# Agent attention and a top-1 mixture of experts in one kernel: the first expert layer issued chunk by chunk, left tiles prepared in sets of two, some VectorE work given to GpSimd, and fewer filler matmuls before the first tile

## The chip, the cores and the metric

The kernel runs on one core of one Trainium2 chip. The metric is device microseconds of one execution; lower is better. Its engines are TensorE (PE, with its weight loads shown as PEld), VectorE (DVE), ScalarE (ACT), GpSimd (POOL) and SyncE (SP, which here issues nearly all DMAs). The program gives each engine its own order of instructions, and they wait on semaphores for one another.

## The reference

The sizes are B = 4 batches, N = 11456 tokens, C = D = 128, 49 agents, E = 8 experts, F = 1024 hidden. Everything is float32.

```python
def sm(a, b):
    s = scale * (a @ b.transpose(0, 2, 1))
    s = s - s.max(-1, keepdims=True)
    e = np.exp(s)
    return e / (e.sum(-1, keepdims=True) + 1e-09)
agent_v = sm(agents, k) @ v            # 49 x 128 for each batch
x = (sm(q, agents) @ agent_v).reshape(B * N, C)
logits = x @ w_gate
e_idx = np.argmax(logits, axis=1)      # one expert for each token
gate_w = softmax(logits)[token, e_idx]
eom = sigmoid(x @ w_output_gate)
for e in range(E):
    mask = e_idx == e
    h = np.maximum(x[mask] @ w1[e], 0.0)
    out[mask] = gate_w[mask, None] * eom[mask, e, None] * (h @ w2[e])
```

## The kernel before

**The work.** A batch is cut into 12 units of 8 columns of 128 tokens (the last has 2 columns of 96), and each unit into one or two *tiles* of 512 tokens: 92 tiles in all. For each batch the kernel first runs over the units of k (scores against the agents, `ks`, and their running maximum), then over those of v (exp of the scores, `ev`; its sum, `sm`; and the product `av`), which gives the 49 averages. `fold` turns them into the weights of the one expert that the batch as a whole prefers, the dominant one: the averages times w1 (`aw`) are split into two float16 parts, `own` and `rest` (tiles `w`), and w2 into `vv`. Then every q unit is scored (`qs`), exponentiated (`ef`), turned by a transposing DMA into `x_ld`, and routed: 8 logits for a token (`lg`), its expert, its gate weight and its output gate (`q_rest`). Every token is sent through the dominant expert, tile by tile. Tokens of another expert are marked on the way (`oht<-oh,ndom`), and worked on again after a phase's batches as *left tiles* of 128 tokens, whose rows replace the first ones: found by counting (`left_table`, `left_index`), gathered from DRAM by indirect DMA, pushed through their own expert in float32 (`let`, `lx`, `lh`, `ly`) and scattered over the output. With these inputs there are 8, 5, 0 and 1 left tiles in the four batches.

**One tile.** Its first layer (`mm1`) makes 8 chunks `h` of 128 hidden values by 512 tokens, in two groups of four. A group takes PSUM banks 0 to 3: four matmuls with `own` (128 rows deep), then four with `rest` (19 rows deep, in four row groups of the array). `relu` follows for each chunk: ACT writes `hh` (float16) and DVE writes what is lost by that, `hl`, and with `hl` the bank is free. The second layer (`mm2`) takes `hh` and `hl` as weights: 8 chunks by 4 columns, each a matmul of 256 columns and one of 128, into banks 4 to 7 (`y`). ACT and DVE add the halves (`ys`, `os`), GpSimd scales (`os<-os,smt`), SP stores.

**What sets the order.** The program is written by a scheduler that runs while the kernel is built. `Clock` holds a model of the time of each engine and of when each buffer is ready; generators (`streams`) each offer their next instruction, and `tick` lets those through that could start by the model's clock, by priority. `main_stream` is the spine: at each step it issues a piece of `mm2`, a whole group of `mm1` if banks 0 to 3 are all free by the model, or, if neither can go, calls `idle`, which lets others through and before the first tile adds a filler matmul (`warm<-idle_x`) if the array has been little used in the last 3413 ns. So what the chip executes is a fixed order for each engine, and where the model was wrong an engine waits, with everything queued behind.

**Before the first tile.** `small_products` goes through `ITEMS`: 12 k units of batch 0, 2 q units, 12 v units, then the q units of batch 0 mixed with k and v of batch 1. `loads` fetches them, 512 KB each, into 8 large places; a place is free once its unit is scored. After each small matmul of these stages `beside` puts a filler of 112 columns into the same PSUM bank (`ks<-idle_x`, `av<-idle_x`, `qs<-idle_x`) until the first tile has started (`clk.started`):

```python
    def beside(t, own):
        if not clk.started:
            PE.matmul(t[:, 512 - SIDE:512], idle_w, idle_x[:, 0:SIDE], start=own, stop=own)
```

**Left tiles.** `PHASES` lists phases as (first batch, batches, left tiles worked on in the main program, table rows). Before, it is batches 0 to 2 with 13 tiles, then batch 3 with 1. `left_prepare` waits until a phase's batches are counted and until the sums of the last batch's v are done, and runs `left_index` twice for the first phase, for 2 tiles and for 11, and once for the second. `left_index` is a chain over SP, DVE and GpSimd: table rows `tbs` and prefix sums into `bigs` by DMA, some twenty small DVE instructions, a gather from `cumd`, more DVE, a gather from `efd`. The order of DVE holds these among the `hl`.

All instructions that go through the recording helpers carry that helper's line, L193 (L203 in the changed kernel), so the profile is read by tile names; buffer and batch numbers are left out of them.

Of the kernel before, what the change touches and what calls it, by code (L numbers as in the profile page):

```python
# [28 lines left out]
PHASES = [(0, 3, 13, 384), (3, 1, 1, 128)]  # L29
NG = B * E  # L30
BIG = 1048576.0
# [17 lines left out]

class Clock:  # L50
# [7 lines left out]
    def __init__(self):  # L58
        self.vt = dict.fromkeys(("PE", "ACT", "DVE", "POOL", "SP", "DMA"), 0.0)
        self.ready, self.read, self.writer, self.before = {}, {}, {}, {}  # L60
        self.slots = [1, 2]
        self.pe = 0.0
        self.psum = set()

        self.apart = {"out"}
        self.recent = []
        self.started = False
# [41 lines left out]
    def issue(self, eng, ins, outs, cost, after):  # L109
        t = max(self.vt[eng], self.at(ins, outs, eng), 0.0 if eng == "PE" else self.now() - 200.0)  # L110
        if eng == "PE":
# [5 lines left out]
            self.pe = 0.0 if wide else cost  # L117
            cost *= slow
# [17 lines left out]
class Engine:  # L136
# [16 lines left out]
    def cost(self, op, ins, outs, k):  # L153
        n = _free(outs[0])
        if self.name == "PE":
# [3 lines left out]
            if not wide and ins[0].shape[0] <= 32:  # L159
                return n / 9.6 + 25.0  # L160
# [82 lines left out]
def agent_attention_top1_moe(ctx, tc, qT, kT, v, aT, wg, wo, w1, w2, cst, out):  # L243
# [51 lines left out]

    def group_free():

        if not all(banks[k][0] for k in range(G4)):
            return None
        return max(when_free(banks[k]) for k in range(G4))  # L300
# [177 lines left out]
    def vacant_turned():  # L478

        return first_place(LARGE, LARGE + SMALL) or first_place(0, LARGE, KEEP)  # L480
# [26 lines left out]
    def loads():  # L507
        for n, item in enumerate(ITEMS):
# [5 lines left out]
            if n == 1:  # L514
                load_constants()

    def beside(t, own):


        if not clk.started:  # L520
            PE.matmul(t[:, 512 - SIDE:512], idle_w, idle_x[:, 0:SIDE], start=own, stop=own)

    def scores(item, name):
# [8 lines left out]
        for t in range(nt):  # L532
            yield from PE.q.matmul(s[0:pp, t * A2:(t + 1) * A2], x[:, t * pp:(t + 1) * pp], at[:, b, :], start=True,
                                   stop=True)
            beside(s, True)
# [8 lines left out]
    def k_unit(b, u):  # L544
        if u == 0:
            K[b] = dict(
                S=wk.tile([P, NCOL, A2], F32, name=f"S{b}", tag="S", bufs=1),
                mx=wk.tile([P, A2], F32, name=f"mx{b}", tag="mx"),
                sm=wk.tile([P, A2], F32, name=f"sm{b}", tag="sme"),
# [5 lines left out]
    def k_rest(b, u, s, mark):  # L555
# [3 lines left out]
        st = sv.rearrange("p (t a) -> p a t", a=A2)  # L559
# [3 lines left out]
        if u == 0:  # L563
            yield from DVE.q.tensor_reduce(mx, st, axis=AX.X, op=ALU.max)
            release(mark)
        else:
            m1 = wk.tile([P, A2], F32, name=f"m1_{b}_{u}", tag="m1")
            yield from DVE.q.tensor_reduce(m1[0:pp], st, axis=AX.X, op=ALU.max)
            release(mark)
            yield from DVE.q.tensor_tensor(mx[0:pp], mx[0:pp], m1[0:pp], op=ALU.max)  # L570
# [4 lines left out]
    def k_max(b):  # L575
        K[b]["M"] = yield from bcast_max(K[b]["mx"], A2, f"km{b}")
# [6 lines left out]
    def v_weights(b, u):  # L583
# [11 lines left out]
        yield from (DVE if b == 0 and u % 3 == 0 else POOL).q.tensor_tensor(e, sv, M[0:pp].unsqueeze(1).broadcast_to([pp, nt, A2]), op=ALU.subtract)  # L595
# [4 lines left out]
    def v_sum(b, u, e):  # L600
        base, pp, nt = UNITS[u]
        sm = K[b]["sm"]
        st = e.rearrange("p t a -> p a t")
        while K[b]["s"] < u:
            yield None
        if u == 0:
            yield from DVE.q.tensor_reduce(sm, st, axis=AX.X, op=ALU.add)
        else:
            m1 = wk.tile([P, A2], F32, name=f"s1_{b}_{u}", tag="m1")
            yield from DVE.q.tensor_reduce(m1[0:pp], st, axis=AX.X, op=ALU.add)  # L610
            yield from DVE.q.tensor_tensor(sm[0:pp], sm[0:pp], m1[0:pp], op=ALU.add)
# [4 lines left out]
    def v_unit(b, u):  # L616
# [12 lines left out]
        for t in range(nt):  # L629
# [3 lines left out]
            if not last_:  # L633
                beside(avp, False)
# [19 lines left out]
    def averages(b):  # L654

        yield from wait_free()
        den = bank(f"den{b}")
        mark = hold()
        yield from PE.q.matmul(den[:, 0:A2], ones, K[b]["sm"], start=True, stop=True)
# [6 lines left out]
    def fold(b):  # L666
# [37 lines left out]
        picking[0] = False  # L704
# [27 lines left out]
        yield from SY.q.dma_start(avnd[b], avn[0:A])  # L732

# [98 lines left out]
    def q_unit(b, u):  # L832
        s, mark = yield from scores(("q", b, u), f"qs{b}_{u}")
        spawn(q_rest(b, u, s, mark))
# [10 lines left out]
    def q_rest(b, u, s, mark):  # L845
# [61 lines left out]
        yield from DVE.q.tensor_tensor(l, L, rr.unsqueeze(2).broadcast_to([pp, nt, 16]), op=ALU.mult)  # L907
# [614 lines left out]
```

## Time and profile before

| | |
|---|---|
| median of 3 runs | 1072.67 us (1071.23 to 1074.8) |
| the profiled execution | 1073.62 us, span of the trace 1071.6 us, mean granted TensorE clock 0.984 |
| busy | PE 1033.2, PEld 840.9, DVE 859.9, ACT 592.6, POOL 275.2 us |
| first `ks` matmul | 7.74 us |
| first `av` matmul, end of the last one | 37.36, 61.2 us |
| first `h` and first `y` matmul | 85.03, 87.7 us |
| last matmul ends | 1060.97 us |
| moved by DMA | 147.13 MB, 137 GB/s in the mean |

Times within the execution count from the trace's first instruction. A row of the timeline gives start, duration, engine, tiles and how many instructions were merged, and in brackets how long the engine was idle before it and who ended that. A row of the windows gives, for a stretch, the busy time and count of each engine, the granted TensorE clock (1 is full, 0.5 half), the busy share of the DMA engines and their GB/s. A float32 matmul shows as two records. Records of matmuls overlap, so how long one takes is the distance from its start to the next start, not its duration.

### The profile page before, as it was taken

The numbers are of one execution on the slowest core, as the hardware profiler recorded it, in microseconds if no ns is written. First come the engines' busy times: TensorE is split into PE (matmuls) and PEld (weight loads), VectorE is DVE, ScalarE is ACT, GpSimd is POOL, SyncE is SP. The second block draws the span as 40 slices with busy tenths as digits, with TensorE's granted clock in tenths as the row PEclk, the third lists the DMA queues.
The fourth block names the chain that finished last, engine by engine and source line by source line (L and its number), as shares of the span: only waits on it lengthen the run. The fifth ranks groups of instructions, "written<-read, shape, count | busy, mean of one in ns | idle before, by whom it ended". The sixth has DMA issues, their size and how long they took to land. (4 is left out here: it accounts for less than half of the span.)

```text
span 1071.6 us, 27654 instructions
## 1 busy us (share of the span) xinstructions
PE 1033.2 (96%) x10671; PEld 840.9 (78%) x10671; DVE 859.9 (80%) x2344; ACT 592.6 (55%) x1396; POOL 275.2 (26%) x440
## 2 busy tenths in 40 slices
PE   9989899999999999999999999999899999999996
PEld 9977777788788877778788788777677676788885
DVE  2738699888988898888988888989989978877551
ACT  2325456565755665556755665556645554655552
POOL 0301123222121232232121232321123263521121
PEclk9999899999999999999999999999999998999998
DMA  8785854444557444453466544446232732644430
GB/s 293 231 213 156 193 117 146 125 122 136 133 141 197 141 134 112 119 147 116 111 185 166 153 125 119 129 123 171 73 75 56 168 92 78 149 136 130 131 124 28
DMA packets 108818, 147.13 MB, mean 137 GB/s; under 512 B 61128, under 2 KB 71548, under 8 KB 108682
## 3 DMA queue, kind: packets, MB, share of 16 engines
q1 hardware_dynamic: 107338, 143.83, 48.4%
q0 software_dynamic: 1344, 1.49, 0.8%
q8 instruction: 85, 1.39, 0.5%
q14 instruction: 51, 0.42, 0.1%
HBM read 91.86 MB, written 35.17 MB: 119 GB/s over the span
## 5 line engine op out<-in xcount | busy, mean ns | idle before, releaser
L193 PE MATMUL y<-vv,hh 128*128 128x256 f16 (+1 forms) x2880 | 593.0, 275 | 4.3 <-DVE w L193 3.1
L193 PE MATMUL y<-vv,hl 128*128 128x128 f16 (+1 forms) x2880 | 532.7, 220 | 3.3 <-DVE hl L193 2.5
L193 DVE SCALAR_TENSOR_TENSOR hl<-h,hh 128x512 f16<-128x512 f32 (+1 forms) x736 | 447.0, 667 | 85.3 <-ACT hh L193 84.2
L193 ACT ACTIVATE hh<-h 128x512 f16<-128x512 f32 (+1 forms) x736 | 372.2, 591 | 231.3 <-PE h L193 231.0
L193 PEld LDWEIGHTS <-hh 128*128 128x128 f16 (+1 forms) x2880 | 284.7, 99 | 67.0 <-issue 37.1
L193 PEld LDWEIGHTS <-hl 128*128 128x128 f16 (+1 forms) x2880 | 320.7, 112 | 10.9 <-DVE hl L193 6.2
L193 PE MATMUL h<-x_ld,w 128*128 128x512 f16 (+1 forms) x1472 | 289.4, 379 | 12.1 <-DVE hl L193 11.5
L193 PEld LDWEIGHTS <-w 128*128 128x128 f16 x1472 | 98.3, 103 | 105.0 <-issue 84.7
L193 POOL TENSOR_TENSOR os<-os,smt 128x512 f32<-128x512 f32 (+1 forms) x92 | 94.3, 1025 | 234.8 <-issue 168.9
L193 ACT COPY ys<-y 128x256 f32<-128x256 f32 x180 | 67.4, 374 | 99.6 <-PE y L193 97.4
L193 PEld LDWEIGHTS qs<-at,q_ld 128*128 128x128 f32 x720 | 112.0, 190 | 7.0 <-DVE km_m L193 0.3
L193 PE MATMUL qs<-at,q_ld 128*128 128x50 f32 x720 | 114.0, 245 | 0.0
L193 PE MATMUL ks<-at,k_ld 128*128 128x50 f32 x720 | 111.4, 257 | 2.2 <-DMA k_ld<-kT 2.2
L193 PEld LDWEIGHTS ks<-at,k_ld 128*128 128x128 f32 x720 | 109.2, 195 | 5.5 <-DMA k_ld<-kT 3.1
L193 PE MATMUL av<-ev,v_ld 128*128 128x50 f32 x720 | 110.7, 251 | 0.0
L193 PEld LDWEIGHTS av<-ev,v_ld 128*128 128x128 f32 x720 | 107.6, 191 | 1.8 <-ACT ev L193 0.2
L193 DVE TENSOR_TENSOR os<-y,ys 128x256 f32<-128x256 f32 x180 | 75.0, 417 | 30.3 <-ACT ys L193 22.4
L193 POOL TENSOR_TENSOR e<-ef,e 128x392 f16<-128x392 f32 (+1 forms) x48 | 41.8, 870 | 151.9 <-ACT e L193 93.4
L193 POOL TENSOR_TENSOR ev<-S,km_o 128x400 f32<-128x400 f32 (+1 forms) x44 | 41.1, 935 | 150.7 <-PE av L193 108.6
L193 POOL TENSOR_SCALAR smt<-lT,i 128x8 f32<-128x8 f32 (+1 forms) x48 | 14.8, 309 | 130.6 <-DVE lT L193 109.9
L193 PEld LDWEIGHTS <-idle_x 128*128 128x128 f16 x305 | 45.9, 158 | 2.7 <-DVE idle_x L193 1.1
L193 PE MATMUL lh<-lxs,lw 128*128 128x128 f32 x224 | 42.9, 276 | 0.0
(200 smaller groups left out, 1041.3 us busy)
## 6 DMA issues: line engine op xcount, KB each, us to landing
q_ld<-qT SPq DMA_DIRECT2D x44, 512.0 KB
v_ld<-v SPq DMA_DIRECT2D x44, 512.0 KB
out<-os SPq DMA_DIRECT2D x88, 256.0 KB
k_ld<-kT SPq DMA_DIRECT2D x43, 512.0 KB
lw<-w SPq DMA_DIRECT2D x28, 512.0 KB
efd<-ef SPq DMA_DIRECT2D x44, 200.0 KB
x_ld<-x_ld SPq DMA_DIRECT2D x176, 38.0 KB
w1t<-w SPq DMA_DIRECT2D x8, 256.0 KB
```

The source lines that it names most:

```text
L193: return getattr(self.eng, op)(*a, **k)
```

## The change

**Fillers and first loads.** `beside` is gone. `filler` puts one matmul of 256 columns into an idle bank after every fourth small matmul until the first tile starts. Loads may run ahead of the first expert choice to item 2 NU + 8 (was + 4), but then stop until the model says that batch 0's w2 has landed (`unpick`). Batch 0's `second`, which squares w2 on ACT, waits until both halves of `w` are written.

**First layer.** `mm1` issues one `own` chunk per call if that one bank is free; the fourth call also issues the four `rest` matmuls. The lead of the first layer over the second, `OFF`, is 10 chunks (was 8).

**DVE and GpSimd.** The maximum of k and the sum of `ev` are kept as 8 x 50 running elementwise maxima and sums and reduced once per batch (`m1`, `s1`); the sums of batches 1 to 3 run on GpSimd, those of batch 0 on DVE. Three of the routing instructions (`ll`, `ld`, `og`) move from DVE to GpSimd. Of batch 0's `ev` subtractions DVE takes every fourth (was third).

**Left tiles.** The phases are now batches 0 and 1 with 13 tiles, and batches 2 and 3 with 1. Indices are made in sets of two tiles, at most two sets alive, in a buffer of their own, and a phase starts as soon as its batches are counted.

**The model.** An instruction of PE, GpSimd or SP that reads what SP loaded is held back another 2000 ns once the first tile has started (`LANDS`); the first `rest` matmul of a group costs 121 ns instead of 25; the last batch's q units may run 8 units ahead (`LAST`, was 5), and q units above 2 of a later batch wait for that batch's `w`.

```diff
-PHASES = [(0, 3, 13, 384), (3, 1, 1, 128)]
+PHASES = [(0, 2, 13, 256), (2, 2, 1, 256)]
+SET = 2
+LANDS = 2000.0
...
-                t = max(t, self.ready.get(x.name, 0.0) + (0.0 if self.writer.get(x.name) in (eng, "PE") else late))
+                w = self.writer.get(x.name)
+                t = max(t, self.ready.get(x.name, 0.0) + (0.0 if w in (eng, "PE") else late + LANDS if late and w == "SP" else late))
...
+    def filler():
+        few[0] += 1
+        if not clk.started and few[0] % 4 == 0:
+            k = idle_bank()
+            if k is not None:
+                PE.matmul(bank("warm", k=k)[:, 0:2 * P], idle_w, idle_x, start=True, stop=True)
...
-        yield from ACT.q.copy(S[0:pp, 8 * u:8 * u + nt, :].rearrange("p t a -> p (t a)"), sv)
-            yield from DVE.q.tensor_reduce(m1[0:pp], st, axis=AX.X, op=ALU.max)
-            yield from DVE.q.tensor_tensor(mx[0:pp], mx[0:pp], m1[0:pp], op=ALU.max)
+        yield from ACT.q.copy(Su.rearrange("p t a -> p (t a)"), sv)
+        if u > 0:
+            yield from DVE.q.tensor_tensor(mx[0:pp, 0:nt], sv.rearrange("p (t a) -> p t a", a=A2),
+                                           S[0:pp, 0:nt, :] if u == 1 else mx[0:pp, 0:nt], op=ALU.max)
...
-            yield from DVE.q.tensor_reduce(m1[0:pp], st, axis=AX.X, op=ALU.add)
-            yield from DVE.q.tensor_tensor(sm[0:pp], sm[0:pp], m1[0:pp], op=ALU.add)
+            yield from (DVE if b == 0 else POOL).q.tensor_tensor(sm[0:pp, 0:nt], sm[0:pp, 0:nt], e, op=ALU.add)
...
+    def unpick(w2t):
+        yield from pause(clk.ready[w2t.name] - clk.now())
+        picking[0] = False
...
+        while b == 0 and len(state[b]["w"]) < 2:
+            yield None
...
-        yield from DVE.q.tensor_tensor(l, L, rr.unsqueeze(2).broadcast_to([pp, nt, 16]), op=ALU.mult)
+        yield from POOL.q.tensor_tensor(l, L, rr.unsqueeze(2).broadcast_to([pp, nt, 16]), op=ALU.mult)
...
-        p = []
-        for g in range(G4):
-            p.append((bank(f"h{i}_{hf}_{g}", k=g), hold()))
-            PE.matmul(p[g][0][:, 0:w], own_[:, g * P:(g + 1) * P], x1, start=True, stop=False)
-            if g < G4 - 1:
-                tick()
+        g = len(group)
+        group.append((bank(f"h{i}_{hf}_{g}", k=g), hold()))
+        PE.matmul(group[g][0][:, 0:w], own_[:, g * P:(g + 1) * P], x1, start=True, stop=False)
+        if g < G4 - 1:
+            tick()
+            return
...
-            if can2 and (G4 * m1 > NB * i + (NB * k + f) / (tiles[i][4] // 2) + OFF or not can1):
+            if can2 and (m1 > NB * i + (NB * k + f) / (tiles[i][4] // 2) + OFF or not can1):
...
-            for i, n in [(0, 2), (2, nst - 2)] if nst > 2 else [(0, nst)]:
+        for i in range(0, nst, SET):
+            n = min(SET, nst - i)
+            sets.append(n)
+            while len(sets) > 2 and sets[-3] > 0:
                 yield None
```

Three places of the built order follow, as they stand in the two programs.

On PE, in the k stage of batch 0, with `ks` the scores and `idle_x` the filler's operand, before:

```order
L193 MATMUL ks_9_458<-at,k_9_ld 128x50
L193 LDWEIGHTS idle_x
L193 MATMUL ks_9_458<-idle_x 128x112
L193 MATMUL ks_9_458<-at,k_9_ld 128x50
L193 LDWEIGHTS idle_x
L193 MATMUL ks_9_458<-idle_x 128x112
```

and now:

```order
L203 MATMUL ks_2_290<-at,k_2_ld 128x50 x4
L203 LDWEIGHTS idle_x
L203 MATMUL warm<-idle_x 128x256
L203 MATMUL ks_2_290<-at,k_2_ld 128x50 x4
L203 LDWEIGHTS idle_x
L203 MATMUL warm<-idle_x 128x256
```

A filler stood beside every small matmul; now one or two stand behind every four. Up to the first `h`, 217 fillers of 112 columns are gone, and fillers of 256 columns go from 52 to 118: the 20 ahead of the first k unit stay, 37 stand in the k stage, 7 among the two q units, 35 in the v stage and 19 behind it. The k, q and v matmuls ahead of the first `h` number 229 before and 228 now.

On ACT, where batch 0's first weights are made (`wsq` squares w1, `vv` with `sq` squares w2, `whi` is the high part of a quarter of the first layer's weights), before:

```order
L193 ACTIVATE wsq_1_1059,sq_945<-w1t_938 128x512
L193 ACTIVATE vv_0_1085,sq_1084<-w2t_941 128x4x128
L193 COPY avn_sb_1082<-avn_1080 49x128
L193 ACTIVATE whi_0_1092<-aw_0_955,s_s 128x512
L193 ACTIVATE vv_1_1087,sq_1084<-w2t_941 128x4x128
L193 ACTIVATE whi_1_1107<-aw_1_1057,s1d_1083 128x512
```

and now:

```order
L203 COPY avn_sb_992<-avn_990 49x128
L203 ACTIVATE whi_0_997<-aw_0_882,s_s 128x512
L203 ACTIVATE whi_1_1011<-aw_1_948,s1d_993 128x512
L203 ACTIVATE whi_2_1017<-aw_2_957,s_s 128x512
L203 COPY S_854<-ks_2_1002 128x400
L203 ACTIVATE whi_3_1031<-aw_3_961,s1d_993 128x512
L203 ACTIVATE vv_0_1049,sq_994<-w2t_872 128x4x128
```

The two squares of w2 stood ahead of and between the `whi`; now they stand behind all four.

On PE in the middle of batch 1, a group of the first layer before (`w_3` is `own`, `w_2` the first `rest`):

```order
L193 MATMUL y_1_8621<-vv_0_4860,hl_1_8368 128x128
L193 LDWEIGHTS w_3_5004
L193 MATMUL h_1_0_8636<-x_7_ld,w_3_5004 128x512
L193 LDWEIGHTS w_3_5004
L193 MATMUL h_1_1_8638<-x_7_ld,w_3_5004 128x512
L193 LDWEIGHTS w_3_5004
L193 MATMUL h_1_2_8642<-x_7_ld,w_3_5004 128x512
L193 LDWEIGHTS w_3_5004
L193 MATMUL h_1_3_8645<-x_7_ld,w_3_5004 128x512
L193 LDWEIGHTS w_2_4979
```

and now, from the second chunk of a group to the third:

```order
L203 MATMUL h_0_1_8696<-x_8_ld,w_1_4786 128x512
L203 LDWEIGHTS hh_7_8445
L203 MATMUL y_1_8628<-vv_1_4557,hh_7_8445 128x256
L203 LDWEIGHTS hl_7_8446
L203 MATMUL y_1_8628<-vv_1_4557,hl_7_8446 128x128
L203 LDWEIGHTS hh_7_8445
L203 MATMUL y_1_8628<-vv_1_4557,hh_7_8445 128x256
L203 LDWEIGHTS hl_7_8446
L203 MATMUL y_1_8628<-vv_1_4557,hl_7_8446 128x128
L203 LDWEIGHTS w_1_4786
L203 MATMUL h_0_2_8704<-x_8_ld,w_1_4786 128x512
```

The four `own` matmuls of a group stood together; now pieces of the second layer stand between them. In the same order the left tiles of the first phase stand between tiles 50 and 79 (of 92), where before they stood from tile 74 to the end; one left tile remains near tile 88.

More of the change, by code (lines that the diff above doesn't have):

```diff
@@ L62, in __init__ @@
         self.pe = 0.0
+        self.rows = False
         self.psum = set()
@@ L515, in loads @@
                 load_constants()
-    def beside(t, own):
-        if not clk.started:
-            PE.matmul(t[:, 512 - SIDE:512], idle_w, idle_x[:, 0:SIDE], start=own, stop=own)
+        loaded.append(True)
+    loaded = []
+    def filler():
[4 more added lines that the diff above has]
+                PE.matmul(bank("warm", k=k)[:, 0:2 * P], idle_w, idle_x, start=True, stop=True)
+    few = [0]
     def scores(item, name):
```

128 lines of the change are left out of this document (64 added, 64 removed).

## The prediction

> **What bounds the kernel now.** I read the page first, then windows over the stages, then the waits of PE, then the timeline wherever one of them pointed. The page's first part names PE:
>
> ```profile
> PE 1033.2 (96%) x10671; PEld 840.9 (78%) x10671; DVE 859.9 (80%) x2344; ACT 592.6 (55%) x1396; POOL 275.2 (26%) x440
> ```
>
> A busy PE is not yet a useful one. Until the first `h` at 85.03 us it computes small matmuls and fillers. The windows of that part, cut at the first `ks` matmul, the first `qs`, the first and last `av`, and the weights (columns: stretch, its length, busy us and count of PE, PEld, DVE, ACT, POOL, granted clock, DMA share, GB/s):
>
> ```profile
> 7.74:31.60 23.86, 23.86 (x272) 23.86 (x271) 7.65 (x19) 5.31 (x13) 1.57 (x4) 1.00 0.90 310
> 31.60:37.36 5.76, 5.59 (x60) 5.15 (x59) 4.37 (x11) 1.61 (x5) 2.01 (x2) 1.00 0.89 310
> 37.36:61.20 23.84, 23.84 (x263) 23.84 (x261) 17.08 (x42) 6.67 (x14) 8.06 (x11) 1.00 0.84 170
> 61.20:69.20 8.00, 7.40 (x90) 6.79 (x89) 4.12 (x23) 1.52 (x6) 0.24 (x1) 1.00 0.30 94
> 69.20:73.30 4.10, 4.09 (x12) 1.82 (x12) 0.96 (x7) 1.19 (x4) 0.00 (x0) 1.00 0.93 314
> 73.30:75.50 2.20, 0.00 (x0) 0.00 (x0) 0.00 (x0) 0.72 (x2) 0.00 (x0) 1.00 1.03 382
> 75.50:85.03 9.53, 9.50 (x68) 8.95 (x69) 7.13 (x19) 5.85 (x12) 1.01 (x2) 0.64 0.91 346
> ```
>
> In the k stage (first row) and the v stage (third row) PE is busy without a gap, so it sets the pace there, with its fillers. After 61.2 the path leaves PE: a chain over DVE, SP's loads of w1, ACT and DVE makes the first weights, and PE idles or runs at a clock of 0.64. From the first `y` at 87.7 to 1060.97 PE is the bound; what can be won there are its waits:
>
> ```profile
> PE h L193 <- DVE hl L193: 11.5, 33, 3.6
> PE lg L193 <- DMA x_ld<-e: 3.7, 1, 3.7
> PE y L193 <- DVE w L193: 3.1, 1, 3.1
> PE ks L193 <- DMA k_ld<-kT: 2.2, 1, 2.2
> ```
>
> **The k and v stages.** The timeline shows what a filler costs there, and a row from mid-run what a small matmul costs alone:
>
> ```profile
> 8.21 0.38 PE L193 MATMUL ks<-at,k_ld 128*128 128x50 f32 x2
> 8.43 0.21 PE L193 MATMUL ks<-idle_x 128*128 128x112 f16 x1
> 8.48 0.38 PE L193 MATMUL ks<-at,k_ld 128*128 128x50 f32 x2
> ...
> 443.70 0.27 PE L193 MATMUL y<-vv,hh 128*128 128x256 f16 x1
> 443.81 0.22 PE L193 MATMUL y<-vv,hl 128*128 128x128 f16 x1
> ...
> 388.55 0.32 PE L193 MATMUL qs<-at,q_ld 128*128 128x50 f32 x2
> 388.70 0.38 PE L193 MATMUL h<-x_ld,w 128*128 128x512 f16 x1
> ```
>
> From 8.21 to 8.48 a small matmul with its filler takes 0.27 us; alone (388.55 to 388.70) it takes 0.15 to 0.16; a matmul of 256 columns takes 0.11 (443.70 to 443.81). Each stage has 90 small matmuls: 90 x 0.27 = 24.3, about the 23.86 and 23.84 of the rows. After, the k stage is 90 x 0.16 + 37 x 0.11 = 18.5 and the v stage 90 x 0.16 + 35 x 0.11 = 18.3, so 5.4 and 5.5 us less. What could be late next is the loads. The DMA engines at their fullest moved this much:
>
> ```profile
> 10.00:15.00 5.00, 5.00 (x58) 5.00 (x58) 1.54 (x4) 1.68 (x5) 0.00 (x0) 1.00 1.03 410
> ```
>
> 512 KB at 410 GB/s is 1.3 us, and a unit of eight matmuls with its three fillers will take 1.6, so PE still sets the pace, narrowly; if the loads got only the 310 GB/s of the k stage's row, a unit would take 1.7 and the two stages would give back some 2 us. The making of `ev` hides too: its subtraction takes 0.99 us on GpSimd, in a row below, which is less than 1.6.
>
> Between the stages lies the chain maximum, transpose, `km_o`, `ev`: the 5.76 us of the second row. The q units' matmuls that cover it shrink, so the chain itself now decides. It gains one reduce per batch:
>
> ```profile
> L193 DVE TENSOR_REDUCE s<-ev 128x50 f32<-128x400 f32 x40 | 33.7, 843 | 2.1 <-ACT ev L193 2.0
> L193 DVE TENSOR_REDUCE m<-ks 128x50 f32<-128x400 f32 x40 | 22.8, 570 | 15.2 <-ACT S L193 15.1
> L193 POOL TENSOR_TENSOR ev<-S,km_o 128x400 f32<-128x400 f32 x40 | 39.6, 991 | 143.8 <-PE av L193 101.7 <-DVE km_o L193 38.7 <-DVE sm L193 2.9
> L193 POOL TENSOR_TENSOR oht<-oh,ndom 128x64 f32<-128x64 f32 x44 | 14.3, 324 | 0.0
> ```
>
> A reduce of 400 elements from SBUF takes 0.84, and about 0.25 is saved on the last unit's own reduce: +0.6. Together the v stage ends 10.3 us earlier, at 50.9.
>
> **From the last av to the first y.** The 8.0 us up to the loaded w1 are a chain and stay; with fewer fillers PE idles in it. Then ACT:
>
> ```profile
> 74.23 0.63 ACT L193 ACTIVATE vv<-w2t 128x512 f16<-128x512 f32 x1 [3.84 <-DMA w2t<-w]
> 76.31 0.68 ACT L193 ACTIVATE whi<-aw,s_s 128x512 f16<-128x512 f32 x1
> ...
> 72.99 0.16 DVE L193 TENSOR_TENSOR s1d<-s_s,kc 128x1 f32<-128x1 f32 x1
> 77.03 0.75 DVE L193 SCALAR_TENSOR_TENSOR w<-aw,s_s,whi 128x512 f16<-128x512 f32 x1 [3.88 <-ACT whi L193]
> ```
>
> The scale was there at about 73.1, and `whi` waited until 76.31 behind a square of w2 that waited for its load. With the squares moved behind, `whi` can start at 73.1; two `whi` (0.68 each, overlapping with DVE) and two `w` (0.75 each) later, at about 75.3, the first group has its weights, against 85.03 before. I put `h` at 75.7 on this old scale, since PE has some 2 us of k matmuls and fillers ahead of it: 9.3 us less. Of that 2.2 come back: `vv` is now late, since its squares, total, scale, ACT and DVE parts (0.63 + 0.63 + 0.7 + 0.4 + 0.65 + 0.75, with hops between) follow the last `whi`, so the first `y` comes 4.9 us behind the first `h`, not 2.67. PE uses 1.3 of these for 8 q matmuls that it owed anyway. Net: 8.4.
>
> The clock takes a part back. After the 2.2 us in which PE had nothing to do (sixth row above), the seventh shows a clock of 0.64, and the idle time ahead of w1 will be as long: about 8.0 minus 5 us of work left there. I charge 2.5 us, half of a 5 us stretch at half clock. The Trainium skill says in "TensorE: Matmul & The Clock Gate", Part 1, that the clock falls only after an idle window of some 3.4 us, and advises against idle gaps over about 3 us; by that the charge would be nothing and the start another 2.5 us shorter. This trace disagrees with it: 2.2 us were enough.
>
> The start, then: 10.3 + 8.4 - 2.5 = **16 us less**, between 8 (PE idle more, loads at 310 GB/s) and 20.
>
> **Waits of the main part.** The 33 waits of `h` for `hl` look like this:
>
> ```profile
> 388.11 0.59 PE L193 MATMUL h<-x_ld,w 128*128 128x512 f16 x2
> ...
> 444.15 0.38 PE L193 MATMUL h<-x_ld,w 128*128 128x512 f16 x1
> 444.75 0.38 PE L193 MATMUL h<-x_ld,w 128*128 128x512 f16 x1 [0.22 <-DVE hl L193]
> ```
>
> Two chunks back to back take 0.59, so 0.21 apart; in a group that was begun before DVE had freed its banks they are 0.60 apart, which loses 0.39 though only 0.22 shows as idle. About 29 of the 33 are of this kind: 11 us. Issued one by one, with second-layer matmuls between, most chunks find their bank free; I keep three quarters, **8 us**, between 2 and 11.
>
> The wait of `lg` for a turned tile (3.7 us, at 123.8) and the half clock behind it fall if the extra 2 us that the model now allows a load are honoured:
>
> ```profile
> 125.00:130.00 5.00, 2.57 (x24) 2.51 (x25) 0.62 (x4) 0.66 (x2) 0.00 (x0) 0.57 0.72 248
> 130.00:135.00 5.00, 5.00 (x41) 3.15 (x40) 3.77 (x14) 2.92 (x8) 0.00 (x0) 0.75 0.70 226
> ```
>
> The clock lost 5 x 0.43 + 5 x 0.25 = 3.4 us, so the place cost 7.1; I take **4** of it, between 0 and 7. For the wait of `y` for `w` (3.1, at the start of batch 3) I find no edit that must remove it: 0.
>
> **Left tiles.** Their index chain puts DVE instructions that wait for a DMA among the `hl`, and PE starves behind them:
>
> ```profile
> 798.02 0.43 DVE L193 TENSOR_TENSOR bigs<-bigs,lrs 128x256 f32<-128x256 f32 x1 [3.41 <-DMA out<-os]
> ...
> 884.61 1.19 DVE L193 TENSOR_TENSOR bigs<-bigs,lppxs 128x990 f32<-128x990 f32 x1 [6.16 <-DMA bigs<-cumd,lrus]
> ...
> 780.00:800.00 20.00, 18.67 (x207) 15.26 (x206) 15.88 (x54) 10.03 (x28) 4.00 (x7) 1.00 0.36 91
> 800.00:820.00 20.00, 17.76 (x163) 12.48 (x163) 17.95 (x57) 10.17 (x24) 6.18 (x10) 0.91 0.25 59
> 880.00:900.00 20.00, 16.13 (x137) 10.79 (x134) 13.40 (x33) 6.75 (x15) 2.54 (x3) 0.83 0.16 45
> 1000.00:1020.00 20.00, 20.00 (x195) 16.65 (x194) 12.40 (x37) 10.62 (x25) 4.00 (x4) 1.00 0.40 131
> ```
>
> The first set (2 tiles) cost 1.33 + 2.24 of idle PE and 0.09 x 20 of clock, 5.4; the set of 11 cost 3.9 + 3.4 = 7.3; the last, of one tile, nothing: 12.7 in all. Now there are eight sets of at most two, each between 0 and 5.4, so 0 to 43. The long wait belonged to eleven gathers in a row, which are gone, and DVE has more room: the 48 units lose a reduce of 0.57 for a maximum of about the same length without the small one behind it, 33 sums of 0.84 and three routing instructions each leave it. I take 1.2 a set, nearer to the set that cost nothing, 10 in all: **3 us less**, between -12.7 and +30.
>
> **GpSimd and the end.** GpSimd gets 33 additions of 0.99 and 144 routing instructions between the 0.32 of `oht` and 0.99, the nearest rows; at 0.4 that is 33 + 58 = 91 us, on top of 275 of 1071. It stays idle two thirds of the time and PE reads nothing of it soon: 0, with the rival below. At the end the last `y` lose the float32 matmuls of left tiles that filled their gaps: +1.5, between 0 and 3.
>
> **Sum.** -16 - 8 - 4 - 3 + 1.5 = -29.5. The page's own execution took 1073.62 us, 0.95 above the median, so 1044.1 there and about **1043 us** as a median. About 0.3% is what a measurement of this kernel can tell from no change.
>
> **Rivals.**
>
> *The start gains little* (15%). The path before the first tile moves from PE to the chains and loads, and the clock halves in the longer gaps. For it: PE is the only thing removed, and the DMA share was 0.84 to 0.90 already. Against it: 410 GB/s were reached. The start gives 8 and the rest 13.5: 1051.
>
> *The stalls go altogether* (15%). Chunk by chunk all 11 us go, the 7.1 of `lg` too, and sets of two cost nothing as the last set of one did (-12.7), with 16 from the start: 16 + 11 + 7 + 12.7 - 1.5 = 45, so 1028.
>
> *DVE waits for others more often* (12%, two thirds of it slower than before). Two edits put waits into DVE's fixed order with `hl` behind them: the eight sets, and routing, where `lm`, `lr` and `ogs` on DVE now read what GpSimd has just written, 144 times. If each set cost the 5.4 of the dearest small one, 43 - 10 = +33; if in addition one hop in twelve starved PE for the 1.33 us of the row at 780, 12 x 1.33 = +16. Then 1043 + 49 = 1092; it turns the sign from +29.5 on. Against it: sets without cost exist, and DVE sheds some 90 us of its 860.
>
> *The chunks do not do what they say* (8%). PE meets the same unfinished `hl` one by one instead of in a group: the 8 us stay, 1051.
>
> The forecast has 50%. Its own range is 1031 to 1057; the stalls' case pulls the lower end down and the DVE case the upper one up, so I give 1022 to 1064. Faster by over 0.3%: all cases but two thirds of the DVE one and a little of the tails, 0.90; within 0.3%: 0.03; slower: 0.07.
>
> **What would show it.** First `h` near 67 and first `y` near 71 to 73 us instead of 85.03 and 87.7; k and v stages of 18 to 19 us with PE busy throughout, or PE waiting for `k_ld` and `v_ld` (then the loads were the bound). `whi` directly behind the scale on ACT. Waits of `h` for `hl` well under 11.5 us. Rows `bigs` on DVE with waits for DMA, and the PE windows around them, tell what the sets cost; waits of DVE for GpSimd's `ll`, `ld`, `og` tell the third rival. I would be wrong if the first `y` came after 80 us, or if the windows between 540 and 800 us showed PE idle by more than a microsecond in twenty.

## The result and the profile after

| | before | after |
|---|---|---|
| median | 1072.33 us (4 runs, 1071.23 to 1074.8) | 1149.15 us (4 runs, 1135.67 to 1151.59) |
| ratio | | 1.069, 95% interval 1.060 to 1.077 |
| profiled execution, clock | 1073.62 us, 0.984 | 1151.59 us, 0.947 |
| first `av`, first `aw` | 37.36, 69.17 us | 37.89, 93.19 us |
| first `h`, first `y` | 85.03, 87.7 us | 101.48, 108.7 us |

The kernel is 77 us slower where 29 faster was forecast. The windows of the start, cut at the same events as before (first `ks`, first `qs`, first `av`):

```profile
7.90:30.40 22.50, 22.50 (x220) 22.34 (x218) 5.17 (x9) 5.55 (x13) 1.57 (x4) 1.00 0.94 338
30.40:37.90 7.50, 6.87 (x47) 6.56 (x47) 5.05 (x11) 2.32 (x6) 3.52 (x4) 0.73 0.69 240
37.90:61.00 23.10, 23.10 (x119) 22.91 (x119) 8.63 (x19) 4.49 (x9) 6.59 (x9) 0.50 0.45 130
61.00:80.00 19.00, 19.00 (x99) 18.82 (x98) 3.82 (x11) 1.36 (x3) 1.76 (x3) 0.50 0.84 164
80.00:93.20 13.20, 13.20 (x81) 13.08 (x81) 3.51 (x20) 1.84 (x7) 0.25 (x1) 0.50 0.48 156
```

The k stage got only 1.4 us shorter, and from the chain behind it the clock stands at one half, with PE busy all the time: the v stage (first to last `av`) takes 42.2 us instead of 23.7. Behind the first `y` the trace runs level with that of before up to 550 us; then come windows like these:

```profile
580.00:600.00 20.00, 13.80 (x153) 12.64 (x153) 8.33 (x29) 6.35 (x18) 3.40 (x6) 0.84 0.58 158
600.00:620.00 20.00, 18.82 (x180) 15.16 (x179) 16.73 (x54) 9.46 (x22) 5.88 (x12) 0.90 0.41 108
620.00:640.00 20.00, 15.02 (x140) 11.34 (x137) 10.56 (x29) 8.61 (x20) 6.77 (x11) 0.83 0.53 175
```

The waits of PE and of DVE name the place, and DVE's timeline shows it. Loads of a left set (`tbs` its table rows, `bigs<-ppid` its prefix sums) hold DVE, with `hl` behind them; GpSimd's routing (`ogs`) holds it for less:

```profile
PE h L203 <- DVE hl L203: 25.6, 25, 4.6
```

```profile
DVE bigs L203 <- DMA bigs<-ppid: 21.8, 8, 4.7
DVE lrs L203 <- DMA tbs<-ttd: 15.8, 4, 5.6
...
DVE ogs L203 <- POOL og L203: 7.5, 8, 2.2
```

```profile
590.84 0.23 DVE L203 TENSOR_SCALAR lrs<-tbs,kc 128x2 f32<-128x2 f32 x1 [4.58 <-DMA tbs<-ttd]
...
596.66 0.42 DVE L203 TENSOR_TENSOR bigs<-bigs,lrs 128x256 f32<-128x256 f32 x1 [3.88 <-DMA bigs<-ppid]
...
599.52 2.47 DVE L203 SCALAR_TENSOR_TENSOR hl<-h,hh 128x512 f16<-128x512 f32 x4
```

To compare kernels I split the stretch from the first `y` to the last: time in which no matmul record runs (idle), half of the busy time inside stretches at half clock, and what is left, the work. The fourth column is the time lost ahead of `own` matmuls of `h`: each one's distance from the matmul ahead of it, less what is usual (the median) for that pair of kinds; it is good to some 3 us.

```
                               length   idle  half clock   work   lost ahead of own h
before                          971.4   23.7      9.3     938.4      19.7
after                          1028.6   53.5     19.7     955.4      57.8
before + chunks                 995.2   39.4     11.7     944.1      54.9
before + eight sets            1006.5   44.0     20.2     942.3      16.8
before + LAST = 8              1007.7   46.6     16.8     944.2      25.8
the best version (below)        959.3   17.6      3.2     938.5       9.0
```

Of the profiled execution's 78 us, 21 lie ahead of the first `y`, and 57 behind it: 30 idle, 10 clock, 17 in the work. What makes up the 17 is open; it may be small waits inside the records. Executions of one program can lie 15 to 24 us apart, by whether the clock halves in the v stage as here (three of these four, by their mean clock); the ratios of single parts below are of executions where it doesn't.

### The profile page after: what moved, and what is told of

It reads as the page before. It is cut to its first block, busy times and chain, and to the rows that moved or that the text cites. A ratio compares the mean times of both kernels' runs of the same rounds, so it can differ in the third digit from the quotient of the medians.

```text
span 1149.8 us, 27405 instructions
## 1 busy us (share of the span) xinstructions
PE 1081.5 (94%) x10520; PEld 876.5 (76%) x10520; DVE 810.0 (70%) x2193; ACT 594.9 (52%) x1396; POOL 353.1 (31%) x627
## 5 line engine op out<-in xcount | busy, mean ns | idle before, releaser
L203 PE MATMUL y<-vv,hh 128*128 128x256 f16 (+1 forms) x2880 | 643.3, 276 | 15.6 <-DVE avs L203 3.8
L203 PE MATMUL y<-vv,hl 128*128 128x128 f16 (+1 forms) x2880 | 560.4, 221 | 0.0
L203 PEld LDWEIGHTS <-hh 128*128 128x128 f16 (+1 forms) x2880 | 294.2, 102 | 107.3 <-issue 70.8
L203 PE MATMUL h<-x_ld,w 128*128 128x512 f16 (+1 forms) x1472 | 338.5, 382 | 30.9 <-DVE hl L203 25.6
L203 PEld LDWEIGHTS <-hl 128*128 128x128 f16 (+1 forms) x2880 | 332.0, 115 | 40.6 <-issue 7.2
L203 PEld LDWEIGHTS <-w 128*128 128x128 f16 x1472 | 92.1, 95 | 57.4 <-issue 50.0
L203 PEld LDWEIGHTS av<-ev,v_ld 128*128 128x128 f32 x720 | 127.6, 230 | 9.6 <-issue 7.3
L203 PE MATMUL av<-ev,v_ld 128*128 128x50 f32 x720 | 127.5, 284 | 0.0
L203 ACT ACTIVATE ev<-ev 128x400 f32<-128x400 f32 (+1 forms) x48 | 25.1, 523 | 37.4 <-POOL ev L203 31.0
L203 PE MATMUL ly<-lw,lh 128*128 128x128 f32 x224 | 42.8, 276 | 0.5 <-DVE os L203 0.5
```

Of the source, the lines that this page charges most:

```text
L203: return getattr(self.eng, op)(*a, **k)
```

## The experiments

Theories: **A**, thin fillers let the clock fall and stay at half; **B**, the sets' loads hold DVE and starve PE; **C**, DVE waits for GpSimd's routing; **D**, chunks hold the banks longer. Three more came later, on the edits of order: **E**, the loads of w1 set when the first weights are made; **F**, the 2 us more for a load (`LANDS`) move instructions into worse places; **G**, the new gates of the q units do it.

**Undoing parts in the changed kernel.** The old fillers again (each small matmul with `beside`, as in the listing of before):

```diff
-            filler()
+            beside(s, True)
```

> The changed kernel with the fillers of before: 112 columns beside every small matmul instead of 256 columns at every fourth. Theory A (thin fillers let the clock fall at 33.9 us and keep it at half up to 95.3): the clock stays at 1.00 through the v stage, the first h comes at 74 to 80 us instead of 101.5, and the time falls by 20 to 27 from 1149 to about 1125, with the stalls from 570 to 900 us left as they are. Rival (the clock falls because of the 0.6 us pause between the stages, whatever fills the rest): the first h stays later than 95 and the time within 5 us of the changed kernel.

Measured: 1136.08 us (1.060, 1.057 to 1.062). In its profile the clock held through the v stage and the first `h` came at 86.3 us (not at 74 to 80, since `aw` waited 6.4 us for its load of w1), but one of its four executions took 1159.83 us, at a mean clock of 0.948 against 0.971 to 0.977. So A is half right: the fillers do not decide it alone. Routing back to DVE:

```diff
-        yield from POOL.q.tensor_tensor(l, L, rr.unsqueeze(2).broadcast_to([pp, nt, 16]), op=ALU.mult)
+        yield from DVE.q.tensor_tensor(l, L, rr.unsqueeze(2).broadcast_to([pp, nt, 16]), op=ALU.mult)
```

(and `ld`, `og` likewise.)

> The changed kernel with the three routing instructions (ll, ld, og) back on DVE. Theory C (DVE waits for GpSimd's routing with hl behind it): the time falls by 15 or more, and the idle time of PE between 570 and 900 us shrinks by a third or more. Theory B (the sets): within 8 us of the changed kernel, the waits for tbs and bigs<-ppid the same in size.

Measured: 1167.13 us (1.083, 1.074 to 1.092), 18 slower than the changed kernel; C fell. Waits of `h` for `hl` grew from 25.6 to 46.6 us. The sets' DVE instructions later, with the thin fillers left in, was to test B alone; its order of instructions ended in a deadlock, so there is no time for it. With the old fillers, the sets' DVE instructions later (by 5 us of the schedule's time) and the sets one after the other:

```diff
+        if nm[0] != "d":
+            yield from pause(5000.0)
         big = wk.tile([P, SET * (2 * P + 12)], F32, name=f"big{nm}", tag="big")
...
+        if nm[0] != "d":
+            yield from pause(5000.0)
         r = col("r")
```

> The changed kernel with the fillers of before and with the later DVE instructions of the sets, both edits at once. Theories A and B together: the gains add, 50 to 70 us, to 1080 to 1100. If the two are one cause (PE's clock, which once low makes every wait longer), less than the sum of the two runs alone by 10 or more.

Measured: 1143.73 us (1.069, 1.064 to 1.073). Up to 570 us each engine's order is that of the run with the old fillers alone, and yet its profile has the clock at half from 35.8 us for 64.9. Between 570 and 960 us DVE's waits for `bigs<-ppid` fell from 17.6 us in that run to 5.7, those for `tbs` from 16.3 to nothing that is listed, and those for `bigs<-cumd` rose from 4.6 to 11.0: part of the wait moves on. From the first to the last `y` it took 1018.1 us instead of 1029.5, so the spreading gained 11 us there, and the clock of the start took them back. Groups of four again, the sets new:

```diff
-    OFF = 10
+    OFF = 8
...
-        group.append((bank(f"h{i}_{hf}_{g}", k=g), hold()))
+            p.append((bank(f"h{i}_{hf}_{g}", k=g), hold()))
```

> The changed kernel with the first layer begun in groups of four again, lead 8, as before. Theory D (chunk by chunk a group of four is spread over 3.4 us instead of 1.3, so 1.8 us instead of 3.6 are left to ACT and DVE to empty its first bank, and every delay of DVE reaches PE): the time lost ahead of own-row h matmuls falls from 58 us to 35 or less, the last rest-row h to the next group's first own-row h grows back to about 3.6 us, and the time falls by 20 or more, to 1130 or less. Theory B alone (the sets' waits are long enough to starve PE either way): the time falls by less than 8.

Measured: 1143.11 us (1.060, 1.054 to 1.066). The time lost ahead of own `h` fell to 9.1 us as D says, the total by only 6. What took its place is not shown: the profiled execution took 1162.46 us, 19 above the median, and has 61.5 us idle in all and 37 lost to half clock.

> The changed kernel with the left tiles as before: phases of three batches and one, sets of 2, 11 and 1 after the last batch's sums. Theory B: the stalls between 570 and 900 us go and those of before (12.7 us) come back, 30 to 45 us less, 1105 to 1120. Theory D: the steady waits of own-row h (14 us in the first 1300 y against 9 before) stay, and the sets' long waits cost more than in the kernel before; the time falls by 15 to 30.

Measured: 1107.62 us, an indication only, since it computes part of the output wrongly. Up to 550 us PE's order is that of the changed kernel, chunks and q edits are in it, and only the left tiles differ; yet the stretch from first to last `y` was 969.8 us, as long as before (971.4), against 1028.6 in the changed kernel. So, as far as this run may be trusted, the sets carry the whole loss behind the first `y` there, and what another part costs depends on the order that it stands in.

> Both: groups of four and the left tiles as before; the start, the fillers, the sums and the routing on GpSimd stay changed. If B and D are the whole cause behind the first y, the time is the kernel before plus what the start costs (15 where the clock stays at half through the v stage, about 0 where not) less what the sums and the routing give: 1065 to 1090. If something else costs there, over 1095.

Measured: 1124.72 us (1.041, 1.033 to 1.049). Over 1095: something else costs. In its profile (1135.17 us, the longest of its four executions) it lay between 740 and 1010 us, far from the start's edits.

**Single parts on the kernel before.** Undoing one of several causes leaves the others to fill its place, so the parts were added singly. Each price below holds for the order of the kernel before.

> The kernel before with one edit, the first layer chunk by chunk with a lead of 10. Theory D: the group's spread grows from 1.3 to about 3.4 us, the time lost ahead of own-row h grows from 20 us to 35 or more, and the kernel is slower by 12 to 30. The forecast on record: 8 us faster (2 to 11).

Measured: 1100.49 us (1.022, 1.017 to 1.027): **24 slower**, D holds. A group of the first layer in this run, and the start of the next:

```profile
441.08 0.38 PE L193 MATMUL h<-x_ld,w 128*128 128x512 f16 x1
...
441.67 0.38 PE L193 MATMUL h<-x_ld,w 128*128 128x512 f16 x1
...
442.27 0.38 PE L193 MATMUL h<-x_ld,w 128*128 128x512 f16 x1
...
443.15 0.71 PE L193 MATMUL h<-x_ld,w 128*128 128x512 f16 x5
...
445.25 0.38 PE L193 MATMUL h<-x_ld,w 128*128 128x512 f16 x1
```

The fourth chunk and its four `rest` matmuls come 2 us behind the first, and only then may ACT and DVE start on the first bank. Over the 184 groups the median from a group's first `own` to its last `rest` grew from 1.28 to 3.06 us, and from there to the next group's first `own` it shrank from 3.63 to 1.82 us, while four `hl` take 2.48. DVE had slack of a microsecond; now its delays reach PE more often (43 waits, 26.1 us, where the kernel before has 33 and 11.5):

```profile
PE h L193 <- DVE hl L193: 26.1, 43, 3.5
```

This run was 15 us behind the kernel before at 477 us. The changed kernel, which has the chunks too but less work on DVE, was level there, and 6 us behind the best version below, so chunks seem to cost less where DVE has room.

The thin fillers alone:

> The kernel before with one edit, the thin fillers (256 columns at every fourth small matmul instead of 112 at each). Theory A: in most executions the clock falls between the k and the v stage and stays at half up to the weights: first h later than 95 us instead of 85.0, the time 8 to 20 above the kernel before; an execution whose clock does not fall there lies within 5 of it. The forecast on record: 10.9 us faster.

Measured: 1075.85 us (1.001, 0.997 to 1.005). Three executions took 1070.82 to 1078.01; in the profiled one, 1092.87, the clock stood at half from 35.5 us for 54.6. The maxima, sums and routing alone:

> The kernel before with the maxima and sums by addition, the sums of three batches and three routing instructions on GpSimd. Theory C (DVE waits for GpSimd in its fixed order): slower by 5 to 20, with waits of DVE for ll, ld and og of 5 us or more. The forecast on record: no cost, since DVE sheds some 90 of its 860 us; by the run with the routing put back on DVE (18 us slower) it may even be 5 to 15 faster.

Measured: two executions of 1068.13 and 1068.65 us, two of 1090.46 and 1090.42; the ratio of the first kind is 0.996 (0.991 to 1.000). C fell again; where the clock holds the part is some 4 us faster, at the edge of what can be told.

> The kernel before with the phases of two and two batches and the eight sets of at most two left tiles. Theory B: DVE waits 20 to 40 us for the rows and gathers of the sets, PE starves between 570 and 900 us, and the kernel is slower by 15 to 40. If groups of four with 3.6 us of slack absorb those waits (theory D), slower by less than 10. The forecast on record: 3 faster.

Measured: 1111.53 us (1.036, 1.031 to 1.041): **39 slower**, B holds and groups of four do not absorb it. The same stretch in this run, and in the kernel before:

```profile
560.00:640.00 80.00, 70.91 (x665) 60.02 (x664) 62.23 (x190) 37.35 (x92) 25.25 (x38) 0.89 0.61 169
```

```profile
560.00:640.00 80.00, 79.77 (x865) 65.31 (x865) 70.86 (x187) 49.47 (x113) 20.50 (x35) 1.00 0.57 150
```

Its waits are of a different make than in the changed kernel:

```profile
DVE bigs L195 <- DMA bigs<-cumd,lrus: 13.6, 6, 3.9
DVE bigs L195 <- DMA bigs<-ppid: 10.7, 6, 3.6
```

> The kernel before with the edits of order around the loads: squares of w2 behind the first weights, more first items, q units held back, 2 us more for a load, the picking flag. The forecast on record: first y 8 us earlier and the wait of lg for a turned tile gone, 8 to 12 faster. Rival: loads that are issued earlier push w1 back, as in the run with the old fillers, where aw waited 6.4 us for it; then the first y is not earlier than 87.7 and the time within 5 of the kernel before.

Measured: 1118.73 us (1.043, 1.040 to 1.046): **46 slower**, by neither expectation. First `y` at 89.4 us, level with before up to 800, lost behind. It was split; first the weights (these lines and `unpick`):

```diff
+        while b == 0 and len(state[b]["w"]) < 2:
+            yield None
```

> The kernel before with one part of the start's edits: the squares of batch 0's w2 behind its first weights, and no other large load until its w2 is there. The forecast on record for this: first y up to 8 us earlier, about 8 us faster. Rival E (the loads of w1 set the first weights, or the clock takes it back): first y within 2 us of 87.7, and the time within 4 of the kernel before.

Measured: 1068.08 us (0.996, 0.995 to 0.998), 3.5 faster. ACT shows why not 8 (row ahead of `whi`; the profiled execution is the longest of eleven, 1077.69 us):

```profile
76.80 0.26 ACT L193 COPY avn_sb<-avn 49x128 f32<-49x128 f32 x1 [5.84 <-PE avn L193]
76.96 0.68 ACT L193 ACTIVATE whi<-aw,s_s 128x512 f16<-128x512 f32 x1
```

> The kernel before with one part: the schedule's model lets whatever reads a loaded tile wait 2 us longer. Theory F (this moves instructions of the left tiles and of the last batch into worse places, and with them the 45 us that the start's edits cost behind 800 us): 30 to 45 slower. Theory G (the q units' new gates do it): within 5 of the kernel before, and the wait of lg for a turned tile at 124 us gone.

`LANDS` alone. Measured: 1073.6 us (1.002, 1.001 to 1.004); F fell.

> The kernel before with one part: q units of later batches held back until the batch's weights are there, the last batch's allowed further ahead, the last two pieces of routing first, four more first loads. Theory G: 30 to 45 slower, lost behind 800 us. Theory F: within 8 of the kernel before.

Measured: 1098.14 us (1.024, 1.022 to 1.027), 26 slower: G. One number of it alone:

```diff
-            while kind == "q" and not roomy(NU * b + u, AHEAD):
+            while kind == "q" and not roomy(NU * b + u, AHEAD if b < B - 1 else LAST):
...
+    LAST = 8
```

> The kernel before with one number: the last batch's q units allowed 8 instead of 5 pieces ahead. If this is what costs the 26 us of the q edits (q units, routing, the large set of left tiles and the last weights then meet at 780 to 960 us): 20 to 30 slower. If the gate on the weights or the order of the first loads does it: within 4 of the kernel before.

Measured: 1110.22 us (1.033, 1.030 to 1.037), **35 slower** from one number, more than with the other q edits around it. Windows restricted to `qs`, before and here, and then the whole of two stretches here:

```profile
700.00:740.00 40.00, 3.15 (x20) 3.15 (x20) 1.60 (x4) 1.00 0.45 136
```

```profile
700.00:740.00 40.00, 10.45 (x66) 9.99 (x65) 3.35 (x8) 0.99 0.56 167
```

```profile
780.00:820.00 40.00, 30.74 (x289) 21.51 (x286) 31.07 (x85) 16.32 (x41) 12.84 (x14) 0.89 0.55 103
820.00:860.00 40.00, 33.95 (x281) 27.23 (x280) 24.13 (x78) 16.50 (x41) 23.08 (x29) 0.81 0.41 109
```

Three times as many q matmuls run at 700 to 740 us, and afterwards no engine is full: PE has 64.7 of 80 us, DVE 55.2. The engines wait for each other in an order that no longer fits. Which instruction of it starts this stays open.

**Versions put together.** The parts that gained, with batch 0 as before:

```diff
+        if b == 0:
+            st = sv.rearrange("p (t a) -> p a t", a=A2)
...
+            yield from DVE.q.tensor_reduce(m1[0:pp], st, axis=AX.X, op=ALU.max)
```

> A version for the end: the kernel before with the routing on GpSimd and the maxima and sums by addition, but batch 0 as before, so that the pause between its k and v stages stays at 0.2 us instead of 0.5 to 0.6. By the run with all of these (4.7 us faster where the clock held, 18 slower where it fell between the stages): 3 to 6 faster than the kernel before, and no execution with the clock at half through the v stage. Rival: the clock falls there by chance and not by that pause; then some executions lie 15 to 20 higher.

Measured: **1061.71 us (0.991, 0.988 to 0.993)**, 10 faster than before, four executions from 1061.17 to 1063.17. It beats both kernels.

> The version of the last call that beat the kernel before (routing on GpSimd, maxima and sums by addition, batch 0 as before), with the weights-first edit added. If the two gains add (9.9 and 3.5 us), 13 faster than the kernel before, about 1058. If the weights-first edit gave its 3.5 us by chance of the order it led to, the same as without it or up to 5 worse, 1061 to 1067.

Measured: 1067.6 us (0.993, 0.991 to 0.995): the gains do not add.

> The changed kernel without its chunks, its eight sets and its q edits: thin fillers, sums and routing on GpSimd, weights first and 2 us more for a load are left. By the single runs (0, 5 faster, 3.5 faster, 2 slower): 1063 to 1070 where the clock holds through the v stage, 15 to 20 more where it falls, and it falls in most executions. Over 1095 if something else in the mixture costs.

Measured: executions of 1063.38, 1065.57, 1080.72 and 1080.81 us beside 1074.99 of the kernel before. So chunks, sets and q edits together are the whole loss, apart from the clock.

**The clock between the stages.** Executions of several kernels fall into two groups, 15 to 24 us apart, by whether the clock halves there (the changed kernel's have mean clocks of 0.947 to 0.954 and, at 1135.67 us, 0.970). PE's pause ahead of `km_t`, in before, the thin fillers alone, the changed kernel and the best version:

```profile
33.32 0.27 PE L193 MATMUL km_t<-kc,mx 128*50 128x128 f32 x1 [0.17 <-DVE mx L193]
```

```profile
31.09 0.27 PE L193 MATMUL km_t<-kc,mx 128*50 128x128 f32 x1 [0.38 <-DVE mx L193]
```

```profile
32.46 0.29 PE L203 MATMUL km_t<-kc,m 128*50 128x128 f32 x1 [0.63 <-DVE m L203]
```

```profile
33.30 0.27 PE L193 MATMUL km_t<-kc,mx 128*50 128x128 f32 x1 [0.17 <-DVE mx L193]
```

With the old chain and fillers (0.17) no execution was of the upper group; with 0.38 (thin fillers) one of four; with 0.48 (sums, old fillers) two of four. Keeping batch 0 as before removed it in ten of ten. But the pause alone does not decide it: in the profile of the run without chunks, sets and q edits PE has the order of the changed kernel up to 89 us and the same pause of 0.63, and the clock held.

What decides it can be read from the 20 profiled executions (all kernels here, one each). Every stretch at half clock is a multiple of 3.41 us long, and within one execution all begin on one grid of 3.41 us; where that grid lies differs from execution to execution. So I cut each execution into these windows and counted the columns that matmuls stream in each. A column counts by the share of the 128 rows that is used, and twice in a float32 record (one of 512 columns takes 0.43 us, a float16 matmul of 256 takes 0.11). The *use* of a window is this count as a share of 2400 columns a us (512 float16 columns take 0.21 us). Of 5981 windows at full clock (from 8 us to the last matmul) 134 were followed by half clock; all but 4 of them had a use under 0.375, and of the other 5847 all but 6 had more. At half clock the same bound holds for the way back: of 134 windows that full clock followed, one had less, and of the 229 others four had more. It is the bound that the `Clock` of the program itself has, 3072 of 8192 columns in 3413 ns.

The window ahead of the fall between the stages had a use of 0.34 to 0.38 in the eight profiles where the clock fell; where it held, no window there had less than 0.40 (the kernel before has 0.405). So the pause and the thin use around it count together, and an edge of the grid decides: the order of the old fillers had 0.42 in two windows with an edge at 34.1 us, and 0.37 in one window in the run with the later sets. In the v stage of the changed kernel a window has a use of 0.50 to 0.52 at full clock (the version without chunks, sets and q edits) and of 0.23 to 0.30 at half, so that a clock that has fallen stays down until other matmuls come.

## Why the prediction was wrong

**The k and v stages: -10.9, failed.** The duration of a small matmul was wrong. It was read at 388.55 to 388.70, where the next matmul was an `h`; in a row of its own kind the rate is another:

```profile
8.84 0.99 PE L203 MATMUL ks<-at,k_ld 128*128 128x50 f32 x8
9.67 0.27 PE L203 MATMUL warm<-idle_x 128*128 128x256 f16 x1
9.78 0.32 PE L203 MATMUL ks<-at,k_ld 128*128 128x50 f32 x2
```

Four (eight records) take 0.83 us, 0.21 each, with PEld busy in 22.34 of the stage's 22.50 us: the float32 weight load probably sets the pace (no run separates it), and the old filler lay mostly beside it. 90 x 0.21 + 37 x 0.11 = 23, and the row says 22.50. At full clock the v stage takes 22.7 (the version without q edits), 1.0 less than before.

**Last `av` to first `y`: -8.4, failed.** `whi` did not wait behind the square alone: `avn_sb` stands ahead of it in ACT's order and waits for PE's `avn`, which PE reaches only behind k matmuls that wait for their load. The listing of ACT's order showed that copy; the working passed over it. In the kernel before (two rows of PE, one of ACT):

```profile
75.53 0.42 PE L193 MATMUL ks<-at,k_ld 128*128 128x50 f32 x2 [2.25 <-DMA k_ld<-kT]
75.84 0.27 PE L193 MATMUL avn<-kc,avd 128*49 128x128 f32 x1
76.15 0.26 ACT L193 COPY avn_sb<-avn 49x128 f32<-49x128 f32 x1 [1.20 <-PE avn L193]
```

Alone the edit brought the first `y` 0.9 us forward, or 1.2 if counted from the first `ks`.

**The clock charge: +2.5, far too small.** The charge stood for idle time behind the v stage, after 2.2 us without work. What came was a stretch of 61.4 us at half clock that began ahead of the v stage, after a pause of 0.63. The step that failed is that idle time was taken for what halves the clock: by the count above it is a window of low use, and in the kernel before too the window from 74.5 to 77.9 us, ahead of the fall that the charge was read from, had a use of 0.37 with 1.0 us of idle time in it. The Trainium skill ("TensorE: Matmul & The Clock Gate", Part 1) puts the fall after an idle window of some 3.4 us and the release after one busy window; neither agrees with this trace, where PE was busy in 6.87 of the 7.50 us around the fall and in all of the 55 that follow at half clock. The first rival (the start gains little) was near it, but kept a gain.

**Waits of `h`: -8, wrong in sign: +24.** "Most chunks find their bank free" failed. The 33 waits were costed as a loss of the group; that the group's bank is held until its `rest` matmuls, and that spreading it takes the time from ACT and DVE, was not. The 24 are the price in the kernel before; in the changed kernel it seems to be smaller, and was not measured singly. The rival for it had 8 us, since it let the chunks at worst change nothing.

**Left tiles: -3, wrong: +39 alone.** The third rival had this mechanism and 33 us for it (eight sets at 5.4), at 8% for the slower outcome. The eight cost 39 more than the three before, which the prediction put at 12.7: 6.5 a set. The value taken, 1.2, leaned on the one set that had cost nothing. Its other half, DVE waiting for GpSimd, did not come as a loss: the changed kernel has such waits (10.9 us for `og`, `ll` and `ld`), but routing and sums on GpSimd gain 4 to 10 us.

**Not priced at all: the q units' lead.** `LAST` stood in the description of the change and in no term of the sum. Alone it costs 35 us, together with the other q edits 26.

**The wait of `lg`: -4, no gain.** With `LANDS` alone the time lost ahead of `lg` fell from 4.9 to 1.3 us, but the time did not (1.002).

**What held:** GpSimd has room, the chain grew as forecast (from the first `qs` to the first `av` 6.3 us with the old fillers, 5.7 before; forecast +0.6), and the two signs named for being wrong (first `y` after 80 us, windows of 540 to 800 with PE idle) both showed. The single parts add to more than 77 us (24 + 39 + 46, less 4, and 15 for the clock): 120. Costs of such parts do not add, and what share of the 57 us behind the first `y` each has in the changed kernel is not shown, beyond the indication that without the sets they were gone.

## What to carry to other kernels

Price a split of grouped work by what the group holds until its last member is issued, and compare the time that is left to the next engine with that engine's work. Give every constant that moves instructions a term, however small it looks; in an order written from a model, one number is a new program and is worth a run by itself. When several parts cost, add them singly to the good version as well as undoing them in the bad one, and do not expect the prices to add.

## What was not expected of the hardware

A pause of PE of 0.4 to 0.6 us was followed, in some executions and not in others of the same program, by 55 to 65 us at half clock although PE had work throughout (four float32 matmuls of 50 columns with one filler of 256, or each with a filler of 112). The matmuls were slower in fact, 1.59 us for four against 0.83. In all 20 profiles the clock goes by how many columns the array streams in each 3.41 us of a grid of its own, with a bound at 0.375 of full use, and not by how long PE is busy. At half clock the same matmuls stream half as many columns, so a mixture of 0.5 that has once fallen cannot climb back: in the changed kernel's profile the clock came back only with the 512-column matmuls of the first weights, at 95.3 us.
